# Pooled attention, then a mixture layer in float32 from float64 weights: the sign bit of the weights set by ScalarE's Prelu, and the first queries loaded in 256-byte pieces and turned by the tensor engine

## The chip, the core and the metric

The kernel runs on one core of a Trainium2 chip. A core has a tensor engine (PE; PEld is its weight load), a vector engine (DVE), a scalar engine (ACT), GpSimd (POOL) and a sync engine (SP) that here issues every DMA. Each engine works off its own instructions in program order; semaphores order them against each other. The metric is the device time of one execution in microseconds (us), lower is better.

## The reference

```python
def _attn_ref(q, k, v):                  # q, k, v: 8 x 8 x 576 x 64, float32
    k_p = k.reshape(B, H, S // 8, 8, D).mean(axis=3)
    v_p = v.reshape(B, H, S // 8, 8, D).mean(axis=3)
    scores = scale * np.matmul(q, k_p.transpose(0, 1, 3, 2))
    scores = scores - np.max(scores, axis=-1, keepdims=True)
    attn = np.exp(scores)
    attn = attn / (np.sum(attn, axis=-1, keepdims=True) + 1e-09)
    return np.matmul(attn, v_p).astype(np.float32)

def _moe_ref(x, w1, w2, w3, w_out):      # x: 4608 x 512
    a = x @ w1
    b = x @ w2
    h = a * b @ w3
    return (h @ w_out).astype(np.float32)
```

The attention's output, with heads side by side, is `x`. The weights are float64: `w1` and `w2` 512 x 1024, `w3` 1024 x 1024, `w_out` 1024 x 512. The kernel folds `w3 @ w_out` into one matrix W of 1024 x 512, since nothing stands between the two products.

## The kernel before

**Weights.** The kernel reads a float64 weight as two 32-bit words. On a raw tile of 128 x 1024 words (512 KB) it builds 128 x 512 float32 values in four instructions:

- `high` (L133, ACT): reads the high word as a float32, multiplies it by 2^-112 with activation Copy and writes z. This leaves sign, exponent and upper mantissa in place, with an exponent field of at most 15, so that its upper bits are clear.
- `low` (L138, DVE): shifts the low word right by 29 into r.
- `conv_b` (L146, DVE): r = (z << 3) | r. The shift drops the sign.
- `conv_c` (L150, DVE): r = (z & top bit) | r. This puts the sign back.

Afterwards each float32 value is split into a rounded part hi and a remainder lo (`split`: a cast on ACT at L154 and a subtraction on DVE or POOL at L155; in `w_block` L187 and L195 cast, L179 and L199 subtract), and each product runs as three passes, hi x hi, hi x lo and lo x hi.

**Order.** The program writes its own order. `at(kind, k, fn, ...)` enters a piece of work at step k; entries are sorted by the whole part of k, then by kind (L loads, P the work around matmuls, M matmuls of the weight and mixture stages, A attention on the tensor engine), then by the fraction of k. Each engine's queue gets its instructions in the order in which the sorted pieces are called. F0 = 4, K0 = 20 and M0 = 36 mark three starts.

**Stages.**

1. Steps 4 to 19: `w_block` turns blocks 0 to 7 of `w3` (s) and the eight row blocks of `w_out` into hi and lo. `w_turn` (L211) transposes a w3 block with four PE transposes. `w_mm` (L571) multiplies, 12 matmuls a block. The loads are in `load_w3` (L120) and `load_wo` (L115); a raw cell of `w3` serves every fourth block.
2. Steps 20 to 35: blocks 8 to 15 of `w3` by `w_conv`, `w_conv2`, `w_conv3` and `w_split`, each at its own step, into the second half of W; beside them the attention of chunk 0.
3. From step 36 (M0): chunks m = 0 to 11 of 384 tokens, 24 steps each. For j = 0 to 7, `a_mm` and `b_mm` (L510, 12 matmuls each) and `out_mm` (L545, 9 matmuls), with `a_post` (L520), `b_post` (L530, L531) and `g_lo` (L536) around them. Beside chunk m runs the attention of chunk m + 1. The 16 tiles of `w1` and `w2` are loaded by `load_w12` (L126) into cells freed by earlier weights, and converted by `w12_conv`, `w12_conv2`, `w12_conv3` and `w12_split` at steps 30 to 53.

**Queries.** The scores need q with the head dimension on the partitions, qT. `load_q` (L276) loads a pair of heads (pr = 0 to 3) in blocks of 32 tokens by 32 columns, 128 bytes contiguous, with four DMAs for a chunk that lies in one batch and eight for one that straddles two (chunk 1). `tr_q` (L287) turns the 32 x 32 blocks with one DVE transpose of 128 x 384. Chunk 0's loads stand at steps 9.5 to 14 and its transposes at 18 to 22.5, chunk 1's at 28.5 to 33 and 30 to 34.5.

**Attention.** `s_mm` (L389) multiplies qT with pooled keys, the soft-max runs in `soft1` (on ACT alone at L415 for some tiles, at L405, L407, L410, L411 on DVE and ACT for others), `soft2` (L424 to L427) and `soft3` (L436, L438), `pt_mm` and `ptr_mm` (L449, L459) transpose, `pt_post` and `ptr_post` (L471, L472, L476) evacuate, `av_mm` (L484 to L487) multiplies with pooled values, and `av_post` (L495, L496) writes xT. Keys and values are pooled by `pool_tree` on POOL (L347 to L349) or by one DVE reduction (L304).

**PSUM.** The pool `patt` has three buffers of one tile tag, att. Every w_turn, s_mm half, transpose and av_mm takes the next one in turn.

Of the kernel before, what the change touches and what calls it, by code (L numbers as in the profile page):

```python
# [8 lines left out]
F32 = mybir.dt.float32  # L9
F32R = mybir.dt.float32r  # L10
I32 = mybir.dt.int32
AF = mybir.ActivationFunctionType
ALU = mybir.AluOpType
# [5 lines left out]
def kernel(  # L19
# [14 lines left out]
    nc = tc.nc  # L34
    ctx.enter_context(tc.manual_schedule())
    B, H, S, D = q.shape
    k_in = k
    P = 128
# [6 lines left out]
    NPR = H // 2  # L45
# [4 lines left out]
    CH = 384  # L50
# [9 lines left out]
    p1 = ctx.enter_context(tc.tile_pool(name="p1", bufs=1))  # L60
# [4 lines left out]
    patt = ctx.enter_context(tc.tile_pool(name="patt", bufs=3, space=PSUM))  # L65


    ident = cp.tile([P, P], F32, name="ident")
# [7 lines left out]
        out=msk,  # L76
        in_=ident.rearrange("p (a two e) -> p two a e", two=2, e=2 * KR),
# [10 lines left out]
    def f(ap):  # L88
        return ap.bitcast(F32)
# [7 lines left out]
    def hl_cell(i):  # L97
        t = cp.tile([P, 2, 512], F32R, tag=f"c{i}", name="hl")
        return t[:, 0], t[:, 1]
# [4 lines left out]
    raw, w3t, wo, w12, W = {}, {}, {}, {}, {}  # L104
    FREED = (8, 0, 9, 1, 10, 2, 11, 3, 12, 4, 13, 5, 14, 6, 15, 7)
    w1r, w2r, w3r, wor = (w.bitcast(I32) for w in (moe_w1, moe_w2, moe_w3, moe_w_out))
    stage = {}
# [21 lines left out]

    def high(c, z):  # L130

        w = c.rearrange("p (c t) -> p c t", t=2)
        nc.scalar.activation(out=z, in_=w[:, :, 1].bitcast(F32), func=AF.Copy, scale=2.0 ** -112)  # L133

    def low(c, r):

        w = c.rearrange("p (c t) -> p c t", t=2)
        nc.vector.tensor_scalar(out=r, in0=w[:, :, 0], scalar1=29, scalar2=None, op0=ALU.logical_shift_right)  # L138

    def conv_a(c, r, z):  # L140
        high(c, z)
        low(c, r)

    def conv_b(r, z):

        nc.vector.scalar_tensor_tensor(  # L146
            out=r, in0=z.bitcast(I32), scalar=3, in1=r, op0=ALU.logical_shift_left, op1=ALU.bitwise_or)

    def conv_c(r, z):
        nc.vector.scalar_tensor_tensor(  # L150
            out=r, in0=z.bitcast(I32), scalar=-2 ** 31, in1=r, op0=ALU.bitwise_and, op1=ALU.bitwise_or)

    def split(src, hi, lo, eng=nc.vector):
        nc.scalar.copy(out=hi, in_=src)  # L154
# [2 lines left out]
    def w_tiles(s):  # L157
        if s == 0:
            stage["wt"] = [t[:, i] for t, x in (
                (p1.tile([P, x, 512], I32, tag=tag, name="wt"), x)  # L160
                for tag, x in (("PTh", 3), ("PTl", 3), ("PTr", 1))) for i in range(x)]
        if s < NJ:
            stage["wo", s] = stage["wt"][s % 4], f(stage["wt"][4 + s % 3])
        stage["w3", s] = W_cell(0, 4 + s % 4, I32), W_cell(1, 4 + s % 4, F32)

    def w_block(v):


        new, mid, old = v < NJ, 0 <= v - 1 < NJ, 0 <= v - 2 < NJ
        if new:  # L170
            w_tiles(v)
            r3, z3 = stage["w3", v]
            ro, zo = stage["wo", v]
            high(raw["w3", v], z3)
            low(raw.pop(("w3", v)), r3)
            high(raw["wo", v], zo)
        if old:
            s = v - 2
            nc.vector.tensor_tensor(out=wo[s][1], in0=f(stage["wo", s][0]), in1=f(wo[s][0]), op=ALU.subtract)  # L179
        if new:  # L180
            if v > 0:
                low(raw["wo", v], ro)
            conv_b(r3, z3)
        if mid:
            ps = w_turn(v - 1)
            w3t[v - 1] = hl_cell(4 + (v - 1) % 4)
            nc.scalar.copy(out=w3t[v - 1][0], in_=ps)  # L187
        if new:
            conv_c(r3, z3)
            if v == 0:  # L190
                low(raw["wo", v], ro)
            conv_b(ro, zo)
        if mid:
            wo[v - 1] = hl_cell(8 + v - 1)
            nc.scalar.copy(out=wo[v - 1][0], in_=f(stage["wo", v - 1][0]))  # L195
        if new:
            conv_c(ro, zo)
        if mid:
            nc.vector.tensor_tensor(out=w3t[v - 1][1], in0=ps, in1=f(w3t[v - 1][0]), op=ALU.subtract)  # L199

# [6 lines left out]
    def w_turn(s):  # L207
        r = f(stage.pop(("w3", s))[0])
        ps = patt.tile([P, 512], F32, tag="att", name="att")
        for it in range(4):  # L210
            nc.tensor.transpose(out=ps[:, it * P:(it + 1) * P], in_=r[:, it * P:(it + 1) * P], identity=ident)  # L211
        return ps
# [5 lines left out]
    def w_conv2(s):  # L218
        conv_b(*stage["w3", s])

    def w_conv3(s):
        conv_c(*stage["w3", s])

    def w_split(s):
        ps = w_turn(s)
        w3t[s] = hl_cell(4 + s % 4)
        split(ps, *w3t[s])
# [10 lines left out]

    def w12_conv2(j, w):
        conv_b(*stage["w12", j, w])  # L240

    def w12_conv3(j, w):
        conv_c(*stage["w12", j, w])

    def w12_split(j, w):
        r, _ = stage.pop(("w12", j, w))
# [4 lines left out]
    def pieces(n):  # L251
        i, r = divmod(n, 3)
        if r == 0:
            return [(2 * i, 0, 384, 0)]
        if r == 1:
            return [(2 * i, 384, 192, 0), (2 * i + 1, 0, 192, 192)]
        return [(2 * i + 1, 192, 384, 0)]

    def tok_tiles(n):
        res = []  # L260
        for (b, s0, cnt, off) in pieces(n):
            step = 128 if cnt == 384 else 96
            for x in range(0, cnt, step):
                res.append((b, off + x, step))
        return res
# [16 lines left out]
    qT = {}  # L282

    def tr_q(n, pr):
        if pr == 0:
            qT[n] = p1.tile([P, NPR, CH], F32, tag="qT", name="qT")
        nc.vector.transpose(  # L287
            out=qT[n][:, pr], in_=stage["q", n][:, pr].rearrange("p n e -> p (n e)"))

    def load_k(b, pr):  # L290
        t = stage["k", b, pr] = st_tile([P, 2, POOL, D])
        nc.sync.dma_start(
            out=t[:KP],
            in_=k_in[b, 2 * pr:2 * pr + 2].rearrange("a (k e) d -> k a (e d)", e=POOL),
        )
# [288 lines left out]
    def at(kind, k, fn, *args):  # L584


        plan.append((k // 1, "LPMA".index(kind), k % 1, len(plan), fn, args))
# [20 lines left out]
    def plan_k(b, k, load, prep, d):  # L608
        for pr in range(NPR):
            at("L", load + 2 * pr, load_k, b, pr)  # L610
            at("P", prep + d * pr, prep_k, b, pr)
        at("A", k, kt_mm, b)
        at("P", k + 1, kt_post, b)

    def plan_v(b, load, load_r, prep, prep2, prep_r):
        for hf in range(2):
            at("L", load + hf, load_v, b, hf)
            at("P", prep + hf, prep_v, b, hf)
            at("P", prep2 + hf, prep_v2, b, hf)
        at("L", load_r, load_vr, b)  # L620
        at("P", prep_r, prep_vr, b)
        at("P", prep_r + 1, prep_vr2, b)

    def plan_q(n, load, d_load, turn, d_turn):
        for pr in range(NPR):
            at("L", load + d_load * pr, load_q, n, (pr,))
            at("P", turn + d_turn * pr, tr_q, n, pr)

    F0 = 4
    K0 = F0 + 2 * NJ  # L630
    M0 = F0 + 2 * NS


    at("L", F0 - 5, warm, 36)
    at("M", F0 - 2, warm, 12)
    for s in range(NJ + 2):
        at("P", F0 + 2 * (s - 2), w_block, s)
    for s in range(NS):
        k = F0 + 2 * s
        if s < NJ:  # L640
            at("L", k - 11, load_w3, s)
            at("L", k - 11, load_wo, s)
        else:
            at("L", k - 14, load_w3, s)
            at("P", k - 7, w_conv, s)
            at("P", k - 6, w_conv2, s)
            at("P", k - 4.5, w_conv3, s)
            at("P", k - 1.5, w_split, s)
        at("M", k, w_mm, s, (0, 1))
        at("M", k + 1, w_mm, s, (2, 3))  # L650
    at("P", K0, w_post, 0)
    at("P", M0 + 0.5, w_post, 1)
    plan_k(0, K0 + 1, K0 - 13.5, K0 - 6.5, 1.5)
    plan_q(0, K0 - 10.5, 1.5, K0 - 2, 1.5)
    plan_v(0, K0 - 4.5, K0 + 5.5, K0 + 2, K0 + 11, K0 + 8.5)
    plan_att(0, [K0 + 3, K0 + 2.5, K0 + 6.5], 0.5, [K0 + 6.5, K0 + 8.5, K0 + 11.5],
             [K0 + 14, K0 + 14.5, K0 + 14.5, K0 + 14.5])
# [2 lines left out]
    for j in range(NJ):  # L660
        for w in range(2):
            i = 2 * j + w
            at("L", K0 + 8.5 + i, load_w12, j, w)
            k = M0 - 6 + 1.25 * i
            at("P", k, w12_conv, j, w)
            at("P", k + 1, w12_conv2, j, w)
            at("P", k + 2, w12_conv3, j, w)
            at("P", k + 4, w12_split, j, w)


    for m in range(NCH):
        m0 = M0 + 3 * NJ * m
        for j in range(NJ):
            k = m0 + 3 * j
# [9 lines left out]
    for n in range(1, NCH):  # L684
        k = M0 + 3 * NJ * (n - 1)
        nt = len(tok_tiles(n))
        s0, pt, av = (3, 5.5, 20.5) if n == 1 else (0, 6, 17) if nt == 4 else (0, 5, 15)
        s_at = [k + s0 + 3 * t for t in range(nt)]
        plan_att(n, s_at, 1, [x + pt for x in s_at], [k + av + pr for pr in range(NPR)])
        if n == 1:  # L690
            plan_q(n, K0 + 8.5, 1.5, K0 + 10, 1.5)
        else:
            plan_q(n, k - 18, 1, k - 9, 1)
    for b in range(1, B):
        k = M0 + 3 * NJ * (3 * (b // 2) + b % 2 - 1)
# [39 lines left out]
```

## Time and profile before

| | us |
|---|---|
| median of three runs | 826.28 (825.61 to 828.12) |
| the profiled execution | 828.94 |
| its span, first to last instruction | 827.2 |

A view of the profile by lines gives groups of equal instructions with their busy time; a view of waits tells for which engine and line another one sat idle; a timeline lists an engine's instructions in order of time (start, duration); a view by windows gives the busy time of each engine in a stretch of time, the clock that PE was granted (1.00 is full), the DMA engines' share of time busy and what they moved. SPq is SP's queue of DMA issues. A matmul in the second stage or later starts each 0.17 to 0.24 us at full clock, while its recorded duration overlaps the next one's.

### The profile page before, as it was taken

How to read it: one execution, taken by the hardware profiler on the slowest of the kernel's cores; microseconds unless marked ns; L12 is line 12 of the kernel's file. 1: busy time of each engine (PE TensorE's matmuls, PEld its weight loads, DVE VectorE, ACT ScalarE, POOL GpSimd, SP SyncE). 2: the span in 40 equal slices, each digit the busy share in tenths (PEclk: the TensorE clock that was granted, in tenths of full speed). 3: DMA queues.
4: the chain of work that ended last, by engine and by line, in shares of the span. 5: the costliest groups of instructions: out<-in, count | busy, mean ns of one | idle time of the engine just before them, and what ended most of it. 6: DMA issues, size and time to landing. Idle time of an engine off the chain costs nothing.

```text
span 827.2 us, 11655 instructions
## 1 busy us (share of the span) xinstructions
PE 784.6 (95%) x4320; PEld 727.5 (88%) x4320; DVE 460.5 (56%) x921; ACT 283.2 (34%) x719; POOL 205.7 (25%) x234
## 2 busy tenths in 40 slices
PE   7877697799999999999999999999999999999998
PEld 6655596699999999999999999999999999999997
DVE  7987999937537436446345355365374374462112
ACT  4535555523224223323233234232243233232211
POOL 2152546601600811105104603006008112000000
PEclk8989988999999999999999999999999999999999
DMA  9996893005304402016014330053034030100101
GB/s 328 214 184 158 223 219 73 1 1 123 88 0 90 108 35 56 1 47 151 16 49 86 77 77 1 0 115 97 1 87 111 25 67 1 39 1 1 40 0 39
DMA packets 113161, 62.64 MB, mean 76 GB/s; under 512 B 80208, under 2 KB 96848, under 8 KB 113104
## 3 DMA queue, kind: packets, MB, share of 16 engines
q1 hardware_dynamic: 113104, 61.89, 30.2%
q8 instruction: 34, 0.56, 0.3%
q14 instruction: 23, 0.19, 0.1%
HBM read 52.43 MB, written 9.44 MB: 75 GB/s over the span
## 4 chain that ended last, share of the span: by engine, by line
PE 80%; DVE 10%; DMA 7%; issue 2%; ACT 1%; SPq 0%; DVEq 0%
PE a L510 23%; PE o L545 23%; PE b L510 23%; PE att L389 4%; DMA raw<-in_moe_w_dram 3%; PE att L449 2%; DMA qs<-in_q_dram 2%; PE att L486 1%; PE att L484 1%; PE att L485 1%; PE att L487 1%; DMA raw<-in_moe_w_out_dram 1%; DVE wb L146 1%; PE att L459 1%; DVE wb L138 1%
## 5 line engine op out<-in xcount | busy, mean ns | idle before, releaser
L510 PE MATMUL a<-xT,hl 128*128 128x384 f32 x1152 | 224.1, 343 | 0.0
L510 PE MATMUL b<-xT,hl 128*128 128x384 f32 x1152 | 221.4, 340 | 0.0
L510 PEld LDWEIGHTS a<-xT,hl 128*128 128x128 f32 x1152 | 206.4, 192 | 4.8
L510 PEld LDWEIGHTS b<-xT,hl 128*128 128x128 f32 x1152 | 200.0, 189 | 0.0
L545 PE MATMUL o<-Wc,gh 128*128 128x512 f32 x576 | 183.6, 400 | 0.0
L530 DVE TENSOR_TENSOR a<-b,a 128x384 f32<-128x384 f32 x96 | 53.1, 554 | 125.8 <-PE b L510 125.7
L545 PEld LDWEIGHTS o<-Wc,gh 128*128 128x128 f32 x576 | 105.1, 189 | 17.3
L347 POOL TENSOR_TENSOR st<-st 72x512 f32<-72x512 f32 (+1 forms) x53 | 75.0, 1415 | 175.2 <-DMA st<-in_k_dram 162.4
L545 PE MATMUL o<-Wc,gl 128*128 128x512 f32 x288 | 114.0, 396 | 0.0
L520 ACT COPY a<-a 128x384 f32<-128x384 f32 x96 | 45.9, 479 | 182.8 <-PE a L510 163.6
L531 ACT CAST gh<-a 128x384 fp32r<-128x384 f32 x96 | 49.2, 512 | 149.0 <-DVE a L530 149.0
L536 DVE TENSOR_TENSOR gl<-a,gh 128x384 fp32r<-128x384 f32 x96 | 62.4, 650 | 34.9 <-ACT gh L531 34.5
L360 POOL TENSOR_TENSOR vbd<-vm,vbd 64x256 fp32r<-64x256 f32 x16 | 13.4, 836 | 253.2 <-ACT vbd L359 248.3
L496 DVE TENSOR_TENSOR xT<-att,xT 128x384 fp32r<-128x384 f32 x48 | 26.6, 556 | 70.8 <-ACT xT L495 70.8
L545 PEld LDWEIGHTS o<-Wc,gl 128*128 128x128 f32 x288 | 54.1, 188 | 12.5
L411 DVE TENSOR_REDUCE sm<-E 128x4 f32<-128x288 f32 (+1 forms) x70 | 31.6, 451 | 46.3 <-ACT E L410 46.3
L571 PE MATMUL o<-hl 128*128 128x512 f32 x144 | 45.3, 455 | 11.0 <-DVE hl L179 10.9
L389 PE MATMUL att<-kbd,qT 128*128 128x144 f32 (+1 forms) x320 | 53.3, 290 | 2.0 <-ACT E L415 2.0
L405 DVE TENSOR_REDUCE mx<-att 128x4 f32<-128x288 f32 (+1 forms) x80 | 35.9, 449 | 29.5 <-PE att L389 29.5
L389 PEld LDWEIGHTS att<-kbd,qT 128*128 128x128 f32 (+1 forms) x320 | 47.4, 182 | 3.1 <-ACT E L415 2.5
L410 ACT ACTIVATE E<-E 128x288 f32<-128x288 f32 (+1 forms) x70 | 31.1, 445 | 55.1 <-DVE E L407 55.1
L571 PEld LDWEIGHTS o<-hl 128*128 128x128 f32 x144 | 30.3, 218 | 19.3 <-DVE hl L179 12.9
(87 smaller groups left out, 850.1 us busy)
## 6 DMA issues: line engine op xcount, KB each, us to landing
raw<-in_moe_w_dram SPq DMA_DIRECT2D x32, 512.0 KB
st<-in_k_dram SPq DMA_DIRECT2D x32, 288.0 KB
out_dram<-ob SPq DMA_DIRECT2D x35, 256.0 KB
st<-in_v_dram SPq DMA_DIRECT2D x32, 256.0 KB
qs<-in_q_dram SPq DMA_DIRECT2D x128, 48.0 KB
raw<-in_moe_w_out_dram SPq DMA_DIRECT2D x8, 512.0 KB
st<-in_v_dram SPq DMA_DIRECT2D x64, 64.0 KB
qs<-in_q_dram SPq DMA_DIRECT2D x128, 24.0 KB
```

The lines of the kernel that those rows point to most:

```text
L347: nc.gpsimd.tensor_tensor(out=t[:, :, 0:4], in0=t[:, :, 0:4], in1=t[:, :, 4:8], op=ALU.add)
L389: nc.tensor.matmul(out=ps[:nt, 2 * KP * j:2 * KP * (j + 1)], lhsT=qT[n][:, pr, off:off + nt], rhs=kbd[b % 2][:, pr], start=True, stop=True,)
L405: nc.vector.tensor_reduce(out=mx[:nt, hs], in_=sv, axis=AX.X, op=ALU.min)
L410: nc.scalar.activation(out=E[:nt, hs], in_=E[:nt, hs], func=AF.Exp, scale=-1.0)
L411: nc.vector.reduce_sum(out=sm[:nt, hs], in_=E[:nt, hs], axis=AX.X)
L510: nc.tensor.matmul(out=o, lhsT=w12[j, w][sw][:, kt * P:(kt + 1) * P], rhs=x[sx][:, kt], start=(i == 0), stop=(i == 3 * NK - 1))
L520: nc.scalar.copy(out=a, in_=gt[m, j][:, :CH])
L530: nc.vector.tensor_tensor(out=g, in0=ps[:, :CH], in1=g, op=ALU.mult)
L531: nc.scalar.copy(out=gh, in_=g)
L536: nc.vector.tensor_tensor(out=gl, in0=g, in1=f(gh), op=ALU.subtract)
L545: nc.tensor.matmul(out=oacc[m][t], lhsT=(gh, gl)[sg][:, c], rhs=W[j][sw], start=(j == 0 and i == 0), stop=(j == NJ - 1 and i == 2))
L571: nc.tensor.matmul(out=wacc[h][it], lhsT=w3t[s][sa][:, it * P:(it + 1) * P], rhs=wo[j][sb], start=(j == 0 and i == 0), stop=(j == NJ - 1 a ...
```

## The change

`high` uses activation Prelu with the same scale and a slope alpha of 2^32 for negative inputs. A negative value thus comes out with an exponent field higher by 32, and the shift by three in `conv_b` moves that bit to the top. `conv_c`, `w_conv3`, `w12_conv3` and their entries in the plan are gone.

Chunks 0 and 1 load q by `load_q3`: partition p gets three consecutive tokens, and for each the 64 columns of one head, 256 bytes; two DMAs per pair of heads for chunk 0, four for chunk 1. `q3_turn` transposes three tiles of 128 x 128 per pair on the tensor engine into an att buffer, and `q3_post` copies them on ACT into qT, with the tokens put back in order. The loads keep their steps. Chunk 0's turns stand at steps 17, 18, 19 and 20, as the last work of the step (kind A); chunk 1's at 32, 33, 35 and 35.5; each copy stands 1.2 steps after the whole part of its turn's step. The other chunks load and turn q as before.

```diff
-        nc.scalar.activation(out=z, in_=w[:, :, 1].bitcast(F32), func=AF.Copy, scale=2.0 ** -112)
+        nc.scalar.activation(out=z, in_=w[:, :, 1].bitcast(F32), func=AF.Prelu, scale=2.0 ** -112, alpha=2.0 ** 32)
...
-    def conv_c(r, z):
-        nc.vector.scalar_tensor_tensor(
-            out=r, in0=z.bitcast(I32), scalar=-2 ** 31, in1=r, op0=ALU.bitwise_and, op1=ALU.bitwise_or)
...
         if new:
-            conv_c(r3, z3)
             if v == 0:
                 low(raw["wo", v], ro)
             conv_b(ro, zo)
...
-        if new:
-            conv_c(ro, zo)
...
+    def load_q3(n, pr):
+        if pr == 0:
+            stage["q", n] = p1.tile([P, NPR, 3, 2, D], F32, tag="qs", name="qs")
+        for (b, s0, cnt, off) in pieces(n):
+            for par in range(2):
+                nc.sync.dma_start(
+                    out=stage["q", n][off // 3:(off + cnt) // 3, pr, :, par],
+                    in_=q[b, 2 * pr + par, s0:s0 + cnt, :].rearrange("(p i) d -> p i d", i=3))
+
+    def q3_turn(n, pr):
+        if pr == 0:
+            qT[n] = p1.tile([P, NPR, CH], F32, tag="qT", name="qT")
+        ps = patt.tile([P, 512], F32, tag="att", name="att")
+        for i in range(3):
+            nc.tensor.transpose(
+                out=ps[:, P * i:P * (i + 1)],
+                in_=stage["q", n][:, pr, i].rearrange("p a d -> p (a d)"), identity=ident)
+        stage["qp", n, pr] = ps
+
+    def q3_post(n, pr):
+        nc.scalar.copy(
+            out=qT[n][:, pr].rearrange("p (c i) -> p i c", i=3),
+            in_=stage.pop(("qp", n, pr))[:, :CH].rearrange("p (i c) -> p i c", i=3))
...
+    def plan_q3(n, load, turn):
+        for pr in range(NPR):
+            at("L", load[pr], load_q3, n, pr)
+            at("A", turn[pr], q3_turn, n, pr)
+            at("P", turn[pr] // 1 + 1.2, q3_post, n, pr)
...
-            at("P", k - 4.5, w_conv3, s)
...
-    plan_q(0, K0 - 10.5, 1.5, K0 - 2, 1.5)
+    plan_q3(0, [K0 - 10.5 + 1.5 * pr for pr in range(NPR)], [K0 - 3, K0 - 2, K0 - 1, K0])
...
-            at("P", k + 2, w12_conv3, j, w)
...
-            plan_q(n, K0 + 8.5, 1.5, K0 + 10, 1.5)
+            plan_q3(n, [K0 + 8.5 + 1.5 * pr for pr in range(NPR)], [K0 + 12, K0 + 13, K0 + 15, K0 + 15.5])
```

More of the change, by code (lines that the diff above doesn't have):

```diff
@@ L219, in w_conv2 @@
         conv_b(*stage["w3", s])
-    def w_conv3(s):
-        conv_c(*stage["w3", s])
     def w_split(s):
@@ L240, in w12_conv2 @@
         conv_b(*stage["w12", j, w])
-    def w12_conv3(j, w):
-        conv_c(*stage["w12", j, w])
     def w12_split(j, w):
```

## The prediction

> **What bounds the kernel now.** I read the page first: busy times, then the span in 40 slices.
>
> ```profile
> span 827.2 us, 11655 instructions
> ...
> PE 784.6 (95%) x4320; PEld 727.5 (88%) x4320; DVE 460.5 (56%) x921; ACT 283.2 (34%) x719; POOL 205.7 (25%) x234
> ...
> PE   7877697799999999999999999999999999999998
> DVE  7987999937537436446345355365374374462112
> ```
>
> PE is the bound over the whole, but not at the start: its holes lie in the first eight slices (20.7 us each), and there DVE is at 7 to 9 tenths. So only about the first 166 us can get shorter. I cut it where the work changes: the end of the first eight weight blocks (56.9), the first matmul of chunk 0 (107.7), and 166.4, the last hole of PE. Busy time by stretch (columns: length, then busy us and count of PE, PEld, DVE, ACT, POOL, then PE's granted clock, DMA share, GB/s):
>
> ```profile
> 0.00:56.90 56.90, 41.63 (x182) 33.61 (x183) 48.67 (x81) 24.12 (x41) 15.75 (x23) 0.85 0.95 245
> 56.90:107.70 50.80, 38.09 (x186) 31.06 (x185) 43.70 (x76) 27.64 (x94) 20.46 (x22) 0.90 0.79 206
> 107.70:166.40 58.70, 48.03 (x250) 44.08 (x249) 55.68 (x92) 30.62 (x93) 37.98 (x26) 0.91 0.39 78
> 166.40:827.20 660.80, 656.82 (x3707) 618.71 (x3706) 312.47 (x675) 200.86 (x492) 131.46 (x163) 1.00 0.21 51
> ```
>
> The last row is full PE at full clock: those 660.8 us stay. In the three before it PE is idle for 166.4 - 41.63 - 38.09 - 48.03 = 38.65 us, while DVE is busy 86%, 86% and 95%. Next come the waits before 170 us, PE's and then two of DVE's own (total us, times, longest):
>
> ```profile
> PE o L571 <- DVE hl L179: 10.9, 5, 5.4
> PE att L484 <- DVE xT L496: 5.7, 1, 5.7
> ...
> DVE hl L155 <- ACT hl L154: 7.1, 3, 2.9
> DVE Wc L138 <- DMA raw<-in_moe_w_dram: 2.9, 2, 2.5
> ```
>
> PE waits for DVE's subtractions, and DVE itself waits little. DVE's queue bounds the first and third stretch, and the second in its latter part. One weight block on DVE's timeline (start, duration) shows why:
>
> ```profile
> 18.62 0.42 DVE L138 TENSOR_SCALAR Wc<-raw 128x512 int32<-128x512 int32 x1
> 18.96 0.69 DVE L179 TENSOR_TENSOR hl<-wt,hl 128x512 fp32r<-128x512 f32 x1
> 19.56 0.42 DVE L138 TENSOR_SCALAR wt<-raw 128x512 int32<-128x512 int32 x1
> 19.89 0.69 DVE L146 SCALAR_TENSOR_TENSOR Wc<-Wc 128x512 int32<-128x512 int32 x1
> 20.61 0.69 DVE L150 SCALAR_TENSOR_TENSOR Wc<-Wc 128x512 int32<-128x512 int32 x1
> 21.22 0.69 DVE L146 SCALAR_TENSOR_TENSOR wt<-wt 128x512 int32<-128x512 int32 x1
> 21.94 0.69 DVE L150 SCALAR_TENSOR_TENSOR wt<-wt 128x512 int32<-128x512 int32 x1
> 22.55 0.69 DVE L199 TENSOR_TENSOR hl<-att,hl 128x512 fp32r<-128x512 f32 x1
> 23.15 0.42 DVE L138 TENSOR_SCALAR Wc<-raw 128x512 int32<-128x512 int32 x1
> ```
>
> Eight instructions without a gap, 23.15 - 18.62 = 4.53 us a block.
>
> **The change part by part.** *conv_c goes.* L150 by stretch, DVE busy and count:
>
> ```profile
> 0.00:56.90 56.90, 14.20 (x19) 0.85 0.95 245
> 56.90:107.70 50.80, 8.01 (x9) 0.90 0.79 206
> 107.70:166.40 58.70, 8.35 (x12) 0.91 0.39 78
> ```
>
> Forty instructions, 30.56 us. A few of them are stretched, and I don't count that part: it comes with POOL's work, which stays and will stretch a neighbour.
>
> *First stretch.* Without its two L150 a block saves 0.72 us twice: each L150 starts 0.72 after the L146 it reads, where independent neighbours start 0.61 apart. That is 4.53 - 1.44 = 3.09 us. PE's own work of a block then matters:
>
> ```profile
> 19.73 0.60 PE L211 MATMUL att<-ident,Wc 128*128 128x128 f32 x4
> 20.09 2.33 PE L571 MATMUL o<-hl 128*128 128x512 f32 x9
> ...
> 22.94 0.60 PE L211 MATMUL att<-ident,Wc 128*128 128x128 f32 x4
> ```
>
> 22.94 - 19.73 = 3.21 us. So the block goes from 4.53 to 3.21 and PE and DVE become even: 1.32 us for each of eight blocks, 10.6. The loads must follow: a block brings 1 MB, and at the 379 GB/s seen below that is 2.8 us, under 3.21. I take **11**, the 0.4 for the slower clock that PE now meets after its 5.4 us wait.
>
> *Second stretch.* From 84.4 to 103.1 DVE has no gap of its own but PE's: four L150 and four transposes lie there, 4 x 0.6 + 4 x 0.5 (start to start) = 4.4 us, straight off the wait of 5.7 us for L496. Before that the soft-max chain on ACT and the waits for L154 hide part of five more L150 and two transposes (4 us): I take three. Together **7.4**; bounds 3 (the tail alone, in part) and 11.4 (8.01 + 3.40). What is late next there is ACT's casts of the av tiles and the soft-max chain.
>
> *Third stretch.* DVE is busy 95% and everything goes through its queue: 12 x 0.61 = 7.3, bounded above by 8.35. PE needs 48.03 of 58.7 at a clock of 0.91, so it isn't the bound after it. I take **7.5**.
>
> *Prelu for Copy.* Same instruction, shape and count on ACT; no row shows a Prelu.
>
> ```profile
> L133 ACT ACTIVATE Wc<-raw x16: 662/674/693, 4.3 to 76.4; 128x512 f32<-128x512 f32 x16
> L133 ACT ACT_TABLE_LOAD  x1: 1283/1283/1283, 0.7 to 0.7; - x1
> ```
>
> Below: nothing to gain. Above: a table load around it, a rival below. I take 0.67 us as now, so 0. That all of Copy, Exp and Copy with scale run behind one load shows one table serving them; it says nothing of Prelu.
>
> *q's loads, transposes and copies.* The eight L287 of chunks 0 and 1 leave DVE (two and six in these stretches):
>
> ```profile
> 0.00:56.90 56.90, 1.13 (x2) 0.85 0.95 245
> 56.90:107.70 50.80, 3.40 (x6) 0.90 0.79 206
> ```
>
> In their place are 24 PE transposes and eight ACT copies from PSUM. By L211 above four transposes take 0.36 us of PE, so three take 0.27, eight times 2.2 us. The copy's nearest row is the 128x384 cast from PSUM:
>
> ```profile
> L495 ACT CAST xT<-att 128x384 fp32r<-128x384 f32 x48 | 22.8, 477 | 43.1 <-PE att L487 43.1
> ```
>
> 8 x 0.48 = 3.8 us on ACT, at 42 to 54% in these stretches: the idle half hides it, and if it didn't, it would delay L154's casts by at most 3.8. The output is strided by three elements, which no row prices; between 0.48 and twice that. Two waits are new: PE's transposes wait for q's DMA, with the turns of w_split and w_mm queued behind them, and ACT's copy waits for PE, with L154's casts behind it. Each turn also takes one of the three att buffers, so PE may wait for DVE to release one. I charge 1 us of PE's 2.2 (the rest falls into its holes) and 1 for waits; bounds 0 and 6.
>
> *q's DMAs*, by SP's timeline (start, duration, count), and by windows (length, PE busy and so on, then clock, DMA share, GB/s) for weights alone, a mix with q, and q alone:
>
> ```profile
> 42.47 1.90 SPq L276 DMA_DIRECT2D qs<-in_q_dram  x4
> 67.21 6.82 SPq L276 DMA_DIRECT2D qs<-in_q_dram  x8
> ```
>
> ```profile
> 10.00:12.00 2.00, 0.00 (x0) 1.00 1.05 379
> 34.00:36.00 2.00, 1.07 (x5) 1.00 1.07 139
> ```
>
> ```profile
> 313.00:314.00 1.00, 1.00 (x6) 0.82 (x6) 0.97 (x3) 0.51 (x1) 0.00 (x0) 1.00 0.62 102
> ```
>
> A pair of heads takes four issues in chunk 0 and eight in chunk 1; it will take two and four, with half the packets at twice the size. The last row lies where SP issues nothing but q. A chunk (384 x 512 x 4 bytes, 786 KB) takes 7.7 us at its 102 GB/s. If a packet's price holds whatever its size, 3.9 us go; if the price goes by bytes, none. That counts only as cover: the loads behind q (w3's later blocks, k, w_in) then keep up with a first stretch shortened by 11 us. If it fails, DMA is late there by up to 4. I charge 1. The Trainium skill speaks against it ("DMA: Bandwidth & Descriptors", Why small descriptors are slow): a packet pays about three cycles beside one per 32 bytes, so 11 for 256 bytes against 2 x 7 for 128; that estimate would save 1.6 us of 7.7 and charge 2 to 3 in place of 1. No run here has shown 256-byte pieces.
>
> The sum: -11 - 7.4 - 7.5 + 1 + 1 + 1 = -22.9. The profiled execution took 828.94 us, its span 827.2; the median of the runs is 826.28, and the span scales to it within 0.1%. So 826.3 - 22.9 = **803.4**.
>
> **The rivals.** *Another engine takes over early* (a smaller gain). With DVE freed, DMA, at share 0.95 in the first stretch, or the soft-max chain in the second binds: the first gives 6, the second 4.4, the third 5, minus 3: 826.3 - 12.4 = 814. For it: PE and DVE would be even in the blocks, and data for early blocks arrive just in time. Against it: DVE waited for weights only 2.9 us.
>
> *A larger gain.* PE's holes close further than the removed work and its clock stays up: a third of the remaining 38.65 - 22.9 = 15.8 goes too, plus 4 of clock: 826.3 - 32 = 794. PE's clock in the weight stretch speaks for it (PE busy alone, clock, share):
>
> ```profile
> 48.00:50.00 2.00, 1.35 (x3) 0.50 1.09 179
> ```
>
> That is half clock right after the 5.4 us wait. The Trainium skill ("TensorE: Matmul & The Clock Gate", Part 1) has it that an idle window of about 3.4 us halves the clock; the trace agrees, and by that rule the matmuls behind a closed hole run at twice the speed. It would move the sum by some 2 us a hole.
>
> *Table loads* (slower). If Prelu isn't in the table that serves Exp, each change between them on ACT reloads. Along ACT's timeline, from the first Exp to the last before 166 us,
>
> ```profile
> 65.86 0.32 ACT L415 ACTIVATE E<-att,mx 128x72 f32<-128x72 f32 x1 [3.10 <-DVE mx L405]
> ...
> 154.58 0.44 ACT L410 ACTIVATE E<-E 96x288 f32<-96x288 f32 x1 [4.79 <-DVE E L407]
> ```
>
> I count 15 changes. A load is 1.283 us by its row; from its start at 0.7 to the first ACTIVATE at 4.3 there are 3.6, which bounds what it can hold up. The gain is eaten from 22.9 / 15 = 1.53 us each, all on the soft-max's path. At the middle, 2.44, the time is 826.3 - 22.9 + 36.6 = 840. The Trainium skill ("ScalarE: Activation LUTs", Table sets) names relu, copy, identity and abs as in every set; Prelu isn't named, and its figure of 2.66 us a switch would give an estimate of 843. One load in the trace can't decide it.
>
> *The pieces bring nothing*: q's DMAs cost as much and PE waits for them at its turns. Then the charges rise from 3 to 8: 808.
>
> **How the numbers follow.** Forecast (798 to 809) 0.55; smaller gain (809 to 818) 0.21; larger gain (789 to 798) 0.12; table loads 0.08; pieces bring nothing 0.04. The likeliest is 803. The range of 8 in 10 leaves out the table loads and the outer half of the larger and of the smaller gain: 794 to 815. What a measurement can tell from no change is 0.3%, some 2.5 us. Faster: all but the table loads and a failed smaller gain, 0.88; within 0.3%: 0.04; slower: 0.08.
>
> **What would show it.** DVE's instructions fall by 48. A weight block takes near 3.2 us and w_mm of block 7 ends near 44 to 46, not 56.9. a's first matmul starts near 90, not 107.7, and PE's last hole ends near 143. One ACT_TABLE_LOAD, L133 still at 0.67 us. PE's waits at the q transposes are under 1 us each. It is wrong if DVE stays as busy with other waits, if PE waits for qs, if DMA stays at share 1 past 60 us, or if table loads appear between Exp and Prelu.

## The result, and the profile after

| | before | after |
|---|---|---|
| median, us | 827.15 (825.61 to 828.12, 4 runs) | 807.99 (805.16 to 809.56, 4 runs) |
| the profiled execution, us | 828.94 | 805.16 |
| its span, us | 827.2 | 803.4 |

The ratio is 0.9759, 95% interval 0.9737 to 0.978: the change takes 19.2 us (18.2 to 21.8). The two profiled executions lie 23.8 us apart, because before's is slower than all four of its runs and after's is the fastest of its four. A sum over this pair of traces therefore overstates the gain by some 4.6 us; in which stretch they lie is not shown.

The page of after, busy times and the two rows of slices that carried the prediction (a slice is now 20.1 us):

```profile
span 803.4 us, 11625 instructions
...
PE 777.9 (97%) x4344; PEld 722.2 (90%) x4344; DVE 431.7 (54%) x873; ACT 288.0 (36%) x727; POOL 196.1 (24%) x234
...
PE   7899888999999999999999999999999999999998
DVE  6968989465373375374374374474454455452112
```

DVE has 48 instructions less (40 `conv_c`, eight transposes), PE and ACT have 24 and eight more. PE's row still has 7 and 8 in the slices 1, 2, 5, 6 and 7: the start got shorter, but it has not become full. The windows of after, cut at the same events (block 7's `w_mm` ends, chunk 0's first `a_mm`, the last hole of PE; columns as before):

```profile
0.00:46.00 46.00, 38.86 (x188) 32.19 (x189) 34.78 (x60) 24.67 (x42) 12.30 (x22) 0.89 0.98 289
46.00:86.70 40.70, 36.79 (x203) 29.94 (x202) 33.78 (x59) 29.09 (x97) 20.79 (x24) 1.00 0.86 222
86.70:144.00 57.30, 46.73 (x251) 42.72 (x249) 52.11 (x82) 32.99 (x98) 31.07 (x26) 0.94 0.50 116
144.00:803.40 659.40, 655.49 (x3707) 617.38 (x3707) 310.99 (x675) 201.21 (x492) 131.96 (x163) 1.00 0.21 51
```

The first stretch went from 56.9 to 46.0 us, the second from 50.8 to 40.7, the third only from 58.7 to 57.3, and the rest is as long as it was. DVE's share in the third is 52.11 of 57.30, still 91%. With 12 `conv_c` of 8.35 us gone from it, its busy time fell by no more than 55.68 - 52.11 = 3.57. The end of the third stretch is a matter of which hole is called the last, so below it is also measured from chunk 0's first `a_mm` to the first `b_mm` of j = 6: 62.3 before, 59.6 after.

Waits of PE before 170 us (total us, times, longest):

```profile
PE att L474 <- ACT E L430: 4.7, 2, 3.9
...
PE o L586 <- DVE hl L177: 3.3, 3, 2.4
...
PE att L499 <- DVE xT L511: 1.6, 1, 1.6
```

L586, L177, L499 and L511 are L571, L179, L484 and L496 of before. The wait for the blocks' subtractions fell from 10.9 to 3.3, that for xT from 5.7 to 1.6. The longest in total is now for the soft-max on ACT; before had it too (L415: 4.1, longest 3.9). One weight block on DVE's timeline (start, duration):

```profile
19.72 0.42 DVE L140 TENSOR_SCALAR Wc<-raw 128x512 int32<-128x512 int32 x1
...
20.99 0.69 DVE L148 SCALAR_TENSOR_TENSOR Wc<-Wc 128x512 int32<-128x512 int32 x1
21.59 0.69 DVE L148 SCALAR_TENSOR_TENSOR wt<-wt 128x512 int32<-128x512 int32 x1
22.30 0.69 DVE L194 TENSOR_TENSOR hl<-att,hl 128x512 fp32r<-128x512 f32 x1
22.91 0.42 DVE L140 TENSOR_SCALAR Wc<-raw 128x512 int32<-128x512 int32 x1
```

A block takes 22.91 - 19.72 = 3.19 us in place of 4.53, and the two independent shifts of L148 now stand 0.60 apart. The new operations on ACT, by source line (busy time of one as least/median/most in ns, then first and last start):

```profile
L135 ACT ACTIVATE Wc<-raw x16: 667/677/745, 4.3 to 62.2; 128x512 f32<-128x512 f32 x16
L135 ACT ACT_TABLE_LOAD  x1: 1283/1283/1283, 0.7 to 0.7; - x1
L301 ACT COPY qT<-att x8: 678/688/723, 42.5 to 87.1; 128x384 f32<-128x384 f32 x8
```

Prelu takes 677 ns where Copy took 674, and there is one table load in the whole span.

**The third stretch, read closely.** The groups that fill POOL and DVE there, before (107.7 to 166.4), as busy us and mean ns of one, then idle time ahead and what ended it:

```profile
L146 DVE SCALAR_TENSOR_TENSOR wb<-wb 128x512 int32<-128x512 int32 x11 | 8.6, 779 | 0.2 <-ACT wb L133 0.2
L138 DVE TENSOR_SCALAR wb<-raw 128x512 int32<-128x512 int32 x11 | 7.7, 699 | 0.0
L155 POOL TENSOR_TENSOR hl<-wb,hl 128x512 fp32r<-128x512 f32 x12 | 24.2, 2025 | 23.2 <-ACT hl L154 18.6 <-DMA qs<-in_q_dram 2.2 <-DMA st<-in_v_dram 1.8
```

and after (86.7 to 144.1):

```profile
L148 DVE SCALAR_TENSOR_TENSOR wb<-wb 128x512 int32<-128x512 int32 x12 | 12.2, 1020 | 0.9 <-ACT wb L135 0.8
L140 DVE TENSOR_SCALAR wb<-raw 128x512 int32<-128x512 int32 x11 | 9.3, 847 | 0.0
L153 POOL TENSOR_TENSOR hl<-wb,hl 128x512 fp32r<-128x512 f32 x12 | 17.8, 1494 | 22.2 <-ACT hl L152 19.9 <-DMA st<-in_v_dram 1.8 <-DVE sm L426 0.5
```

Nothing in these six groups was edited, and all of them moved. POOL's twelve subtractions got shorter by 24.2 - 17.8 = 6.4 us. DVE's `conv_b` got longer by 0.24 each and its `low` by 0.15: 12 x 0.24 + 11 x 0.15 = 4.5 us. Other rows of DVE moved as well, some down (L427 from 5.4 to 4.7) and some up (L536 from 2.7 to 3.5), so the balance is that of all of DVE: 8.35 us were removed and 3.57 gained. Single instructions show the exchange. Before, on POOL's timeline and then on DVE's:

```profile
114.62 4.92 POOL L155 TENSOR_TENSOR hl<-wb,hl 128x512 fp32r<-128x512 f32 x1 [1.49 <-ACT hl L154]
```

```profile
114.77 0.67 DVE L150 SCALAR_TENSOR_TENSOR wb<-wb 128x512 int32<-128x512 int32 x1
115.37 0.68 DVE L146 SCALAR_TENSOR_TENSOR wb<-wb 128x512 int32<-128x512 int32 x1
115.96 0.55 DVE L536 TENSOR_TENSOR gl<-a,gh 128x384 fp32r<-128x384 f32 x1
```

and after:

```profile
124.41 1.28 POOL L153 TENSOR_TENSOR hl<-wb,hl 128x512 fp32r<-128x512 f32 x1 [5.85 <-ACT hl L152]
127.11 1.60 POOL L153 TENSOR_TENSOR hl<-wb,hl 128x512 fp32r<-128x512 f32 x1 [1.42 <-ACT hl L152]
```

```profile
123.85 0.69 DVE L148 SCALAR_TENSOR_TENSOR wb<-wb 128x512 int32<-128x512 int32 x1 [0.77 <-ACT wb L135]
124.46 1.52 DVE L140 TENSOR_SCALAR wb<-raw 128x512 int32<-128x512 int32 x1
...
127.47 1.78 DVE L148 SCALAR_TENSOR_TENSOR wb<-wb 128x512 int32<-128x512 int32 x1
```

Before, this subtraction of POOL lasts 4.92 us, while DVE's instructions beside it, a `conv_c` first among them, run at their usual length (0.67, 0.68 and 0.55 here). It is the longest of 13; the median is 1.29 us in both kernels, and the longest of after is 2.69. After, POOL is through in 1.28 and 1.60, and DVE's `low` and `conv_b` beside it take 1.52 and 1.78 in place of 0.42 and 0.69. One of the two engines seems to wait for the other. The experiments ask what that costs, and where the rest of the forecast went.

### The profile page after: what moved, and what is told of

Read it like the earlier page. It is cut to its first block, busy times and chain, and to the rows that moved or that the text cites. A ratio compares the mean times of both kernels' runs of the same rounds, so it can differ in the third digit from the quotient of the medians.

```text
span 803.4 us, 11625 instructions
## 1 busy us (share of the span) xinstructions
PE 777.9 (97%) x4344; PEld 722.2 (90%) x4344; DVE 431.7 (54%) x873; ACT 288.0 (36%) x727; POOL 196.1 (24%) x234
## 4 chain that ended last, share of the span: by engine, by line
PE 85%; DVE 7%; DMA 4%; issue 2%; ACT 2%; SPq 0%; DVEq 0%
PE o L560 24%; PE a L525 24%; PE b L525 23%; PE att L404 4%; PE o L586 2%; DMA st<-in_k_dram 2%; PE att L464 2%; DVE wb L140 1%; DVE wb L148 1%; PE att L501 1%; PE att L500 1%; PE att L502 1%; PE att L499 1%; PE att L474 1%; DMA raw<-in_moe_w_out_dram 1%
## 5 line engine op out<-in xcount | busy, mean ns | idle before, releaser
L362 POOL TENSOR_TENSOR st<-st 72x512 f32<-72x512 f32 (+1 forms) x53 | 73.0, 1377 | 173.2 <-DMA st<-in_k_dram 161.0
L551 DVE TENSOR_TENSOR gl<-a,gh 128x384 fp32r<-128x384 f32 x96 | 59.4, 619 | 35.8 <-ACT gh L546 35.4
L511 DVE TENSOR_TENSOR xT<-att,xT 128x384 fp32r<-128x384 f32 x48 | 26.5, 556 | 70.0 <-ACT xT L510 70.0
L586 PE MATMUL o<-hl 128*128 128x512 f32 x144 | 42.3, 430 | 3.3 <-DVE hl L177 3.3
L363 POOL TENSOR_TENSOR st<-st 72x256 f32<-72x256 f32 (+1 forms) x53 | 41.8, 789 | 4.2
```

Of the source, the lines that this page charges most:

```text
L362: nc.gpsimd.tensor_tensor(out=t[:, :, 0:4], in0=t[:, :, 0:4], in1=t[:, :, 4:8], op=ALU.add)
L363: nc.gpsimd.tensor_tensor(out=t[:, :, 0:2], in0=t[:, :, 0:2], in1=t[:, :, 2:4], op=ALU.add)
L551: nc.vector.tensor_tensor(out=gl, in0=g, in1=f(gh), op=ALU.subtract)
L586: nc.tensor.matmul(out=wacc[h][it], lhsT=w3t[s][sa][:, it * P:(it + 1) * P], rhs=wo[j][sb], start=(j == 0 and i == 0), stop=(j == NJ - 1 a ...
```

## The experiments

All ratios are to the kernel before, on the same chip; differences between two variants are differences of their medians. Four runs of after spread over 4.4 us, so a difference of one or two microseconds says nothing here. The kernel before had medians from 825.99 to 827.85 beside these runs; by the ratios the differences from after given below as 4.3, 4.4, 9.0, 3.0 and 4.3 are 4.1, 6.0, 9.3, 4.0 and 5.5.

### One part at a time

Prelu alone: after, with the queries as before.

```diff
-    plan_q3(0, [K0 - 10.5 + 1.5 * pr for pr in range(NPR)], [K0 - 3, K0 - 2, K0 - 1, K0])
+    plan_q(0, K0 - 10.5, 1.5, K0 - 2, 1.5)
...
-            plan_q3(n, [K0 + 8.5 + 1.5 * pr for pr in range(NPR)], [K0 + 12, K0 + 13, K0 + 15, K0 + 15.5])
+            plan_q(n, K0 + 8.5, 1.5, K0 + 10, 1.5)
```

> Prelu without conv_c, but all queries loaded in 128-byte pieces and transposed on DVE as before. Theory A (each piece of DVE work is worth what lies on DVE's queue, the queries only their eight transposes): 811 to 813, since eight transposes are 4 us of DVE and about 3 of them lie on the path. Rival B (the shortened blocks need the faster query loads, DMA binds otherwise): 815 to 819, with PE or DVE waiting for DMA before 60 us. Rival C (the queries bring nothing): 808.

Measured: 812.26, ratio 0.9808 (0.9787 to 0.9829), 4.3 above after. DVE's waits before 150 us:

```profile
DVE Wc L140 <- DMA raw<-in_moe_w_dram: 6.3, 5, 2.4
...
DVE qT L276 <- DMA qs<-in_q_dram: 5.5, 2, 4.6
```

With the blocks shortened, DVE's transposes wait 5.5 us for the queries' small pieces; L138's wait for weights in before was 2.9. PE then waits 8.0 us for xT, in after 1.6, and chunk 0's first `a_mm` starts at 94.5, not 86.7.

The queries alone: before, with `load_q3`, `q3_turn`, `q3_post` and `plan_q3` in place of `plan_q` at the two places (the edit above, the other way round, in the kernel before).

> Copy and conv_c as before, chunks 0 and 1 with 256-byte pieces and PE transposes. A: 823 to 825, 2 to 4 us under before, all of it in the second stretch. B: the same or less, since the blocks then run at the old pace and the old loads kept up: 826 to 827. C: 827.

Measured: 828.74, ratio 1.001 (0.9996 to 1.0024): nothing. Yet chunk 0's first `a_mm` starts at 103.4, not 107.7. By the first `b_mm` of j = 6 the lead is 170.0 - 168.8 = 1.2 us: it is used up in the third stretch, which takes 65.5 us from `a_mm` to that `b_mm`.

To see whether the new copies' place on ACT does that, the last two copies of chunk 1 were put a step later, behind the casts of `w12_split`.

```diff
-            at("P", turn[pr] // 1 + 1.2, q3_post, n, pr)
+            at("P", turn[pr] // 1 + (2.2 if n == 1 and pr > 1 else 1.2), q3_post, n, pr)
```

> The queries' part alone (Copy and conv_c as before) with chunk 1's last two copies one step later. In the run of the queries alone the first matmul of chunk 0 came 4.4 us earlier and the gain was gone 20 us later, and DVE idled 2.9 us behind ACT's wait for PE. If that wait took the gain: 823 to 826. If DVE's and POOL's queue in the third stretch takes it whatever the order on ACT: 827 to 829.

Measured: 828.22, ratio 1.0007 (0.9992 to 1.0022). The stretch still takes 65.4 us. The order on ACT is not what uses the lead up. The same edit on after:

> The changed kernel with chunk 1's last two copies into qT one step later on ACT, behind the casts of W's second half. In the changed kernel ACT sits idle 1.7 us before these copies, until PE has turned the tiles, and the casts, DVE's subtractions and POOL's queue behind them wait. If that wait is on the path: 1 to 3 us under the changed kernel, 805 to 807. If DVE's queue swallows it: 808.

Measured: 805.26, ratio 0.9736 (0.9709 to 0.9762). That is 2.7 us under after by the medians and 1.9 by the ratios. The intervals overlap, so this is inconclusive.

The new queries, with each 256-byte piece as two of 128, and so with twice the DMAs:

```diff
-                nc.sync.dma_start(
-                    out=stage["q", n][off // 3:(off + cnt) // 3, pr, :, par],
-                    in_=q[b, 2 * pr + par, s0:s0 + cnt, :].rearrange("(p i) d -> p i d", i=3))
+                for d0 in (0, 32):
+                    nc.sync.dma_start(
+                        out=stage["q", n][off // 3:(off + cnt) // 3, pr, :, par, d0:d0 + 32],
+                        in_=q[b, 2 * pr + par, s0:s0 + cnt, d0:d0 + 32].rearrange("(p i) d -> p i d", i=3))
```

> The changed kernel with each of its 256-byte pieces loaded as two of 128 bytes (twice the issues and packets, same layout and same turns). If the packets' number is what the queries' loads cost: 2 to 5 us above the changed kernel, 810 to 813, with PE waiting for qs or DVE for raw weights. If the pieces' size brings nothing: 808.

Measured: 812.40, ratio 0.9831 (0.9809 to 0.9853), 4.4 above after and level with Prelu alone. DVE's waits now have a line that after lacks:

```profile
DVE wb L140 <- DMA raw<-in_moe_w_dram: 5.9, 3, 3.5
```

The tiles of w1 and w2 come behind chunk 1's queries in SP's queue, and now come late. So what the queries' part gives hangs on its bigger pieces, or on its half as many DMAs, which this edit doesn't tell apart. That DVE transposes less and PE more makes no difference to the time that these runs show, only to where the lateness strikes: here chunk 0's first `a_mm` starts at 88.3, but the stretch from it to the `b_mm` of j = 6 takes 64.2 us, where Prelu alone has 94.5 and 58.7, and after 86.7 and 59.6. The queries' part is worth something only with the shorter stretches ahead, 4.3 us there and nothing in the kernel before.

### `conv_c` put back, one stretch at a time

In `w_block` (16 instructions; the helper `conv_c` returns unchanged in all three):

```diff
         if new:
+            conv_c(r3, z3)
             if v == 0:
...
+        if new:
+            conv_c(ro, zo)
```

> The changed kernel with conv_c kept in the eight blocks (16 instructions; with Prelu its result is the same). A (DVE's queue binds the blocks, 1.3 us each): 10 to 12 us above the changed kernel, 818 to 820, w_mm of block 7 ending near 57. Rival (DMA or PE would have bound the blocks anyway): under 814.

Measured: 817.02, ratio 0.9872 (0.9853 to 0.9891): 9.0 above after, one microsecond short of the first expectation. Block 7's `w_mm` ends at 57.3, as in before (56.9), not at 46.0.

For blocks 8 to 15 of w3 (8 instructions):

```diff
+            at("P", k - 4.5, w_conv3, s)
```

> The changed kernel with conv_c kept for blocks 8 to 15 of w3 alone (8 instructions in the second stretch; the result is the same). Forecast as recorded (most of them lie on the path): 4 to 5 us above the changed kernel, 812 to 813. Rival (PE, at full clock and 90% busy there now, binds the second stretch): 0 to 2 us, 808 to 810.

Measured: 811.01, ratio 0.9807 (0.9789 to 0.9825): 3.0 above after, between the two expectations.

For w1 and w2 (16 instructions):

```diff
+            at("P", k + 2, w12_conv3, j, w)
```

> The changed kernel with conv_c kept for w1 and w2 alone (16 instructions, four of them in the second stretch, twelve in the third). Forecast as recorded (each is worth 0.6 us): 9.7 us above the changed kernel, 817 to 818. Theory D (in the third stretch the removed instructions were given back, because DVE now waits for POOL where POOL waited for DVE): 2 to 5 us above, 810 to 813, with DVE's remaining conversions shorter on average and POOL's subtractions longer, near 2.0 us each where the changed kernel has 1.5.

Measured: 812.31, ratio 0.9825 (0.9803 to 0.9847): 4.3 above after. POOL's subtractions there, by lines, 89.4 to 151.1 us:

```profile
L157 POOL TENSOR_TENSOR hl<-wb,hl 128x512 fp32r<-128x512 f32 x12 | 24.4, 2039 | 19.5 <-ACT hl L156 16.7 <-DMA qs<-in_q_dram 2.2 <-DVE sm L433 0.6
```

With these sixteen instructions back (three of them ahead of this window), POOL's subtractions are back at 2.04 us, as in before (2.03), from 1.49. DVE's two rows in the same window:

```profile
L148 DVE SCALAR_TENSOR_TENSOR wb<-wb 128x512 int32<-128x512 int32 x12 | 10.3, 862 | 0.2 <-ACT wb L135 0.2
L140 DVE TENSOR_SCALAR wb<-raw 128x512 int32<-128x512 int32 x11 | 7.7, 697 | 0.0
```

They got shorter again, from 1.02 to 0.86 and from 0.85 to 0.70. So the removal of `conv_c` from DVE is what shortened POOL's subtractions and lengthened DVE's own rows. The stretch from `a_mm` to the `b_mm` of j = 6 takes 63.9 us in place of 59.6.

### POOL's subtractions

The 13 subtractions of `w12_split` on POOL were taken out. The part of the computation that this leaves out is the low part of those 13 tiles; the passes that would use it run on the high part, with the same matmuls.

```diff
-        split(f(r), *w12[j, w], eng=nc.vector if (j, w) in LO_DVE else nc.gpsimd)
+        if (j, w) in LO_DVE:
+            split(f(r), *w12[j, w])
+        else:
+            nc.scalar.copy(out=w12[j, w][0], in_=f(r))
+            w12[j, w] = (w12[j, w][0], w12[j, w][0])
```

In after:

> The changed kernel without the 13 subtractions on POOL that form the low part of w1 and w2; the high part stands in for the low one, so the product's remainder is wrong. DVE, ACT and PE keep their instructions. Theory D (DVE waits for POOL's instructions in the third stretch): the stretch shrinks by 4 to 8 us, 800 to 804, and the conversions L148 there go from 1.02 us on average towards 0.69. Rival E (DVE's own queue and the soft-max's order set the third stretch, POOL is beside the path): 807 to 809, with L148 shorter or not.

Measured: 792.37, ratio 0.9583 (0.9566 to 0.96). That is 15.6 us under after by the medians and 14.5 by the ratios, far more than either expectation had. DVE by lines, 84 to 134 us:

```profile
L148 DVE SCALAR_TENSOR_TENSOR wb<-wb 128x512 int32<-128x512 int32 x12 | 9.3, 777 | 0.9 <-ACT wb L135 0.8
L140 DVE TENSOR_SCALAR wb<-raw 128x512 int32<-128x512 int32 x11 | 7.3, 662 | 0.0
```

L148 went from 1.02 to 0.78 and L140 from 0.85 to 0.66, on an engine whose own instructions are the same. The stretch from `a_mm` to the `b_mm` of j = 6 takes 48.1 us in place of 59.6.

In before, the same edit:

> The kernel before without the thirteen subtractions on POOL (the high part of w1 and w2 stands in for the low one, so the remainder is wrong). Theory D': POOL's price was smaller while DVE's queue was longer and POOL waited for DVE: 5 to 10 us under before, 817 to 822. If POOL's price was there all along: 12 to 17 us under before, 810 to 815, and then it doesn't explain why the change gained less in the third stretch than forecast.

Measured: 815.67, ratio 0.9864 (0.9845 to 0.9883): 11.3 us, between the two expectations. Taken together: with POOL's subtractions the change is worth 19.2 us, without them 815.67 - 792.37 = 23.3. The subtractions cost 11.3 in before and 14.5 to 15.6 in after. The windows from chunk 0's first `a_mm` to the first `b_mm` of j = 6 tell how much of this lies in the third stretch (columns as above), in before, after, and the same two without the subtractions:

```profile
107.74:170.03 62.29, 51.62 (x262) 47.71 (x261) 58.16 (x97) 32.20 (x97) 38.72 (x27) 0.89 0.37 73
86.74:146.31 59.57, 49.00 (x265) 44.98 (x263) 54.28 (x87) 34.42 (x102) 31.50 (x27) 0.94 0.48 111
```

```profile
105.22:156.75 51.53, 47.81 (x263) 45.20 (x261) 46.92 (x96) 31.97 (x97) 15.83 (x15) 0.91 0.39 82
85.55:133.60 48.05, 45.49 (x265) 41.76 (x263) 43.70 (x85) 34.45 (x102) 14.23 (x18) 1.00 0.66 162
```

Two things follow. First, the change shortens this stretch by 62.29 - 59.57 = 2.7 us with the subtractions and by 51.53 - 48.05 = 3.5 without them; the other 105.2 - 85.6 = 19.7 lie ahead of it. So the forecast's 7.5 does not come back when the subtractions go. PE is then busy 93% and 95% of the stretch, which leaves little to gain. DVE's busy time again falls by only 46.92 - 43.70 = 3.22: POOL's pooling steps, which stay, now stand beside DVE. One of them takes 4.97 us in before without the subtractions, and by the change DVE's `conv_b` goes from 0.71 to 0.78 there and `low` from 0.54 to 0.66.

Second, without the subtractions DVE's busy time falls by 11.24 us in before and by 10.58 in after, and the stretch by 10.8 and 11.5. In before it is not the shifts alone that were stretched. Two more of DVE's rows, in before and then in before without the subtractions:

```profile
L427 DVE TENSOR_TENSOR E<-E,sm 96x576 f32<-96x576 f32 x4 | 5.4, 1356 | 0.1
L424 DVE TENSOR_SCALAR sm<-sm 96x8 f32<-96x8 f32 x4 | 4.0, 992 | 0.0
```

```profile
L431 DVE TENSOR_TENSOR E<-E,sm 96x576 f32<-96x576 f32 x4 | 3.0, 754 | 0.1
L428 DVE TENSOR_SCALAR sm<-sm 96x8 f32<-96x8 f32 x4 | 0.6, 162 | 0.6 <-ACT E L419 0.6
```

The waits of PE and of its weight load name POOL's low parts nowhere in before's trace and for 0.2 us in after's, so in these two their later arrival does not show as a wait.

All sixteen subtractions on DVE, nothing left out:

```diff
-    LO_DVE = [(0, 1), (4, 1), (6, 0)]
+    LO_DVE = [(j, w) for j in range(8) for w in range(2)]
```

> The changed kernel with all sixteen subtractions of w1 and w2 on DVE (thirteen of them leave POOL); the result is the same. DVE gets 13 x 0.61 = 7.9 us. Theory D (a subtraction on POOL costs DVE and PE more than one on DVE): leaving them out gave 15.6, so 798 to 804. Rival E (DVE's work sets the third stretch): 812 to 816.

Measured: 801.60, ratio 0.9696 (0.9673 to 0.9718), 6.4 under after by the medians and 5.2 by the ratios. DVE by lines, 85.4 to 139.7 us:

```profile
L153 DVE TENSOR_TENSOR hl<-wb,hl 128x512 fp32r<-128x512 f32 x13 | 10.2, 783 | 5.1 <-ACT hl L152 5.0
L148 DVE SCALAR_TENSOR_TENSOR wb<-wb 128x512 int32<-128x512 int32 x12 | 8.7, 725 | 0.0
L140 DVE TENSOR_SCALAR wb<-raw 128x512 int32<-128x512 int32 x11 | 4.6, 417 | 0.0
```

`low` is back at 0.42 us and `conv_b` at 0.73: these two groups cost DVE 12.2 + 9.3 - 8.7 - 4.6 = 8.2 us less than in after. The eleven subtractions that it takes over in this window cost it 10.2 - 1.9 = 8.3. Other rows got shorter too: from chunk 0's first `a_mm` to the `b_mm` of j = 6 DVE is busy 47.61 us with 97 instructions, where after has 54.28 with 87, and the stretch takes 56.5 us in place of 59.6.

With the later copies as well:

> The same with chunk 1's last two copies one step later. If ACT's wait for PE at these copies is on the path, 1 to 3 us under the run with the subtractions alone; if not, the same as it.

Measured: 799.95, ratio 0.9684 (0.9662 to 0.9707). It is the fastest version that computes everything, 8.0 under after by the medians (6.2 by the ratios) and 3.2% under before; from the one without the later copies it can't be told apart.

## Why the prediction was right, and where a size was off

The forecast was 803 (794 to 815), faster; the median is 807.99. The terms against what the traces and the runs give:

| term | forecast | pair of traces (23.8 in all) | one part put back |
|---|---|---|---|
| first stretch | 11 | 10.9 | 9.0 |
| second stretch | 7.4 | 10.1 | 3.0 for `conv_c`, 4.3 for the queries in both chunks |
| third stretch | 7.5 | 2.7 | 4.3 |
| charges | -3 | in the above | in the above |

The last column adds up to 20.6, against 19.2 measured; by the ratios it is 22.9 against 19.9. The third stretch's 4.3 is the price of all sixteen `conv_c` of w1 and w2, of which three lie ahead of it.

In part the number was luck. Without the charges the forecast takes off 25.9 us, and the parts put back give 20.6: the 3 us of charges covered about half of what the first and the third stretch fell short by. That the rival "the pieces bring nothing" had 808, the very time measured, is a coincidence, since here they bring 4.4.

1. **First stretch: right.** The block is 3.19 us (forecast 3.21, PE's own work), block 7's `w_mm` ends at 46.0 (44 to 46), and the wait for L179's subtractions fell to 3.3. The loads did follow, at 289 GB/s over the stretch and a DMA share of 0.98: close to its limit.
2. **Second stretch: the sign and the place right, the mechanism only in part.** Chunk 0's first `a_mm` starts at 86.7 (forecast near 90), and the wait for xT fell from 5.7 to 1.6. But I booked four of DVE's transposes at 2 us there. Their removal, with the new turns and copies in their place, is worth nothing that shows (812.40 against 812.26); q's larger pieces, or their fewer DMAs, are. The granted clock went from 0.90 to 1.00 in this stretch, which I had left to the rival of a larger gain.
3. **Third stretch: the mis-sized term.** The step was "DVE is busy 95% and everything goes through its queue: 12 x 0.61 = 7.3". It gave 2.7 by the pair of traces and 4.3 by putting `conv_c` back. DVE's queue did bind, but its instructions have no fixed price there. POOL's subtractions stood waiting while DVE ran; with twelve instructions less on DVE, POOL got in sooner, and DVE stood in its place: 8.35 us removed, 3.57 gained. I had seen the stretching and set it aside as "POOL's work, which stays". The work stayed, but who pays for it changed. Putting `conv_c` back turned both sides round (POOL's subtractions 1.49 to 2.04, `conv_b` 1.02 to 0.86, `low` 0.85 to 0.70). Taking POOL's subtractions out did not bring the 7.3 back: the change then gives 3.5 there, with PE busy 95% and POOL's other steps still beside DVE. That its whole gain, 23.3, is near the forecast sum of 22.9 is therefore no support for this term.

   The Trainium skill has the mechanism ("SBUF — State Buffer", Who interferes with whom): DVE and GpSimd share one pair of ports under an exclusive lock, a DVE instruction with two inputs in SBUF contends with a GpSimd instruction that reads there, and the order of issue decides who is blocked. The trace agrees that either can be the one that waits: POOL's 4.92 beside short DVE instructions before, DVE's 1.78 beside POOL's 1.60 after. It doesn't show the part on the order. By the recorded starts POOL is first in all three cases (114.62 against 114.77 before, 124.41 against 124.46 and 127.11 against 127.47 after), and yet before it is POOL that waits, through a whole row of DVE's instructions.
4. **Prelu at no cost: right, and the table-load rival is out.** 677 ns against 674, and one load. The Trainium skill ("ScalarE: Activation LUTs", Table sets) does not name Prelu; here it shares its table with Exp and Copy.
5. **The charge for DMA cover: right about the mechanism.** I had written that if the cover fails, DMA is late by up to 4 us. With 128-byte pieces in twice the DMAs it fails, and costs 4.4. The rival that the pieces bring nothing holds in the kernel before (ratio 1.001) and not in after. What one packet costs at 256 bytes against 128 was not measured by itself, so my figure and the estimate from the Trainium skill stay undecided.
6. **The charge for the new waits: unresolved.** A copy into qT takes 0.69 us in place of the 0.48 of its nearest row, within the bound of twice that. Moving two of them changed nothing that the runs can tell. PE nowhere waits for q's DMA in after: ahead of the turns PE and its weight load sit idle 1.1 us for xT and 0.5 for an evacuation on ACT.
7. **The rival "another engine takes over early" is right that the gain is smaller, at 814 too small, and wrong about the place.** It put DMA and the soft-max chain ahead. The DMA share of 0.98 does show, and PE's 3.9 us wait for ACT's E is as long as before; but the largest shortfall against the forecast is in the third stretch, between DVE and POOL.

Open: why without the subtractions the change is worth some 4 us more by the medians when the pair of traces doesn't show it (23.2 against 23.8); what the third stretch would give with nothing on POOL at all; and why the queries' lead of 4.3 us is lost in the kernel before, since the place of the copies on ACT does not explain it.

## What to carry to other kernels

When a row of an engine's instructions varies in length, look at what its neighbour runs at those moments: removing work from it can let the neighbour in first, so the gain has to be sized by what the engine's whole busy time loses (here 3.57 us of the 8.35 removed), not by the removed row. Moving work to an idle engine can cost the busy one more than doing it would: here 13 subtractions of 0.78 us on DVE beat the same on an engine busy 24% of the time by 5 to 6 us. A better load can be worth nothing alone and, as here, 4 us once the stretch ahead of it is shortened, so test such parts together and each alone.

## What the hardware showed beyond that

- An instruction with a single tile as input is stretched too: `low` takes 0.42 us when DVE does the subtractions itself, 0.66 as a mean without POOL's subtractions but with its other work, and 1.52 at 124.46 in after, right behind the start of one of POOL's. The extra time (1.10) is about what POOL's subtraction still had to run (124.41 + 1.28 - 124.46 = 1.23).
- A copy from PSUM of 128 x 384 whose output steps by three elements took 688 ns, where the contiguous cast of the same shape took 477 (L495 of before) and the copy of L520 479.
